# The first block's queries and keys loaded by head pairs in 2 KB rows, and turned by 64-column matmuls

## Chip, cores and metric

One core of a Trainium2 chip. The metric is device time in microseconds (us). The profiled span is about 1.8 us shorter than the device time of the same run, so differences may be read from either. In the lines of the profile PE is TensorE (PEld its weight loads), DVE is VectorE, ACT ScalarE, POOL GpSimd and SP SyncE; a load "lands" when its last count is posted.

For a program on one core, a run more than 1.5% above the fastest of the same kernel is called slow, and a difference of less than 2% is called "same".

## The reference

Attention over the last 128 positions and the first 4 ("sinks"), then a two-layer network on its result.

```python
# q, k, v: (4, 8, 768, 64) float32; w_in: (512, 2048); w_out: (2048, 512)
scores = q @ k.transpose(0, 1, 3, 2) / sqrt(64)
rel    = pos[:, None] - pos[None, :]
keep   = (pos[None, :] < 4) | ((rel >= 0) & (rel < 128))
a      = softmax(where(keep, scores, -1e9))
x      = (a @ v).transpose(0, 2, 1, 3).reshape(3072, 512)
h      = x @ w_in
out    = (h / (1 + exp(-1.702 * h))) @ w_out
```

## The kernel before

The 3072 tokens are worked on in 12 blocks of 256. For each block q and k are loaded, cast to fp16 and turned, so that the head dimension lies on the partitions; then come scores, exponentials, the product with v, and the two layers. A list scheduler inside the kernel puts all operations into one order per engine, using estimated durations. It also fills early gaps of TensorE with "warming" matmuls on zeros, which keep its clock up: between 14 and 16 us the granted clock is 0.50 in the changed kernel, and 1.00 in run 4, which adds more of them.

Block 0's q goes through SP's ring (its list of transfers) and its k through ACT's, each in two loads of 256 KB:

```python
def load(k):
    ...
    for e, src in enumerate((q, k_ap)):
        eng, dma = ("ACT", nc.scalar) if k == 0 and e else ("POOL", nc.gpsimd) if k == 2 else ("SP", nc.sync)
        if k < KT:                            # KT = 4: blocks 0 to 3
            for h in range(2):                # even heads, odd heads
                dma.dma_start(                # (called through the scheduler)
                    dst[:, e].rearrange("p h i d -> p (h i d)")[:, 512 * h : 512 * h + 512],
                    src[b, h::2, t0 : t0 + TB].rearrange("p (g i) d -> g p (i d)", i=8),
                )
    ... # v of the block, then the next block, behind these in SP's ring
```

Eight tokens of one head are contiguous in memory: 8 x 64 x 4 bytes = a row of 2 KB. In the source pattern `g` is the group of eight tokens (32 of them) and `p` the head of the half (4). Destination partition 4g + p takes one row. Each half, once cast, holds the even or odd heads alone, and turning works on an even and an odd head side by side, so it waits for both halves:

```python
def turn_on_pe(k, e, i, T, C, war):
    def tp():
        for a in range(4):                    # 128 columns: two heads of 64
            nc.tensor.transpose(f16(o_tp)[:, bass.ts(a, P)], C[:, a].rearrange("s h d -> s (h d)"), perm)
    o_tp = op("PE", ..., tp, [o_cqk[k, e, 0], o_cqk[k, e, 1], o_perm], ...)   # both halves
    ... # copies from PSUM to blkT, on DVE or ACT
```

`perm`, the identity with its columns in another order, undoes the order of the partitions. It is the moving operand; the data are what PE loads as weights (`LDWEIGHTS <-qk` in the trace).

The softmax here doesn't subtract the row's maximum and nothing guards it: scores larger than these inputs give would overflow.

## Time and profile before

Three runs gave 221.77 us (median; 221.62 to 227.12). The start, by when things happened in the profiled run (us from its start; landings from the semaphore records):

| event | us |
|---|---|
| block 0 lands: k half 1, q half 1, k half 2, q half 2 | 4.66, 5.33, 6.37, 7.04 |
| last cast of block 0 starts | 7.06 |
| first exponential starts | 9.44 |
| v of block 0, v of block 1 land | 11.73, 14.06 |
| first weight transfer lands | 16.41 |
| first matmul with w_out starts | 28.81 |
| end of the span | 220.0 |

The lines of the profile are in the prediction below.

### The profile page before, as it was taken

To read this page: it belongs to the slowest core of one execution; us is meant where nothing else is said; L and a number is where in the kernel's file an instruction comes from. 1 tells how busy PE (TensorE), PEld (TensorE's weight loads), DVE (VectorE), ACT (ScalarE), POOL (GpSimd) and SP (SyncE) were. 2 spreads that over 40 slices of the span, in tenths; PEclk is the share of its full clock that TensorE was granted. 3 is DMA by queue.
4 is the path that set the end of the run, shared out by engine and by line. 5 is a ranking of instruction groups with operands and counts; after the bars stand their busy time and mean duration, and the time that the engine had idled before them with its cause. 6 is when DMAs were issued, how large, how long until landed. Compare 5 with 4: busy or idle time off the path is not lost.

```text
span 220.0 us, 5209 instructions
## 1 busy us (share of the span) xinstructions
PE 213.7 (97%) x2066; PEld 143.8 (65%) x2066; DVE 125.9 (57%) x274; ACT 125.7 (57%) x243; POOL 87.0 (40%) x150
## 2 busy tenths in 40 slices
PE   7889999999999999999999999999999999999993
PEld 3448777577757766666666667657667666666642
DVE  2678855397826855656556664666465655634310
ACT  2597645777557576475485476466466486444320
POOL 2596431689971956704905727508500000000000
PEclk9999999999999999999999999999999999999998
DMA  5999999999979589289498589398541312231223
GB/s 162 355 236 204 207 302 202 324 302 289 210 141 240 143 182 295 51 166 297 103 205 240 73 204 250 84 213 232 106 91 47 71 27 48 52 68 26 51 48 95
DMA packets 65911, 36.54 MB, mean 166 GB/s; under 512 B 27968, under 2 KB 61120, under 8 KB 65888
## 3 DMA queue, kind: packets, MB, share of 16 engines
q1 hardware_dynamic: 60848, 30.19, 56.0%
q0 software_dynamic: 4592, 5.37, 12.9%
q10 hardware_dynamic: 448, 0.66, 1.1%
q8 instruction: 16, 0.26, 0.5%
q14 instruction: 7, 0.06, 0.1%
HBM read 27.56 MB, written 6.29 MB: 154 GB/s over the span
## 4 chain that ended last, share of the span: by engine, by line
PE 91%; DMA 4%; ACT 2%; SPq 1%; issue 0%; DVE 0%
PE bank L736 39%; PE bank L765 37%; PE bank L669 6%; PE bank L604 5%; DMA qk<-in_q_dram 3%; PE bank L532 1%; DMA out_dram<-osb 1%; ACT at L629 1%; ACT v L286 1%; PE bank L596 1%; PE bank L584 1%; PE bank L708 1%; SPq L407 0%; PE bank L846 0%; ACT blkT L286 0%
## 5 line engine op out<-in xcount | busy, mean ns | idle before, releaser
L765 PE MATMUL bank<-w_out,gT 128*128 128x512 f16 (+2 forms) x400 | 99.8, 371 | 0.0
L736 PE MATMUL bank<-xT,w_in 128*128 128x256 f16 x768 | 99.8, 273 | 0.0
L750 DVE SCALAR_TENSOR_TENSOR gT<-th,bank 128x512 f16<-128x512 f16 x96 | 65.5, 683 | 48.8 <-ACT th L748 47.8
L748 ACT ACTIVATE th<-bank 128x512 f16<-128x512 f32 x96 | 57.7, 603 | 62.0 <-PE bank L736 61.3
L736 PEld LDWEIGHTS <-w_in 128*128 128x128 f16 x768 | 72.9, 98 | 23.8 <-issue 1.7
L286 POOL CAST qk<-qk 64x512 f16<-64x512 f32 (+1 forms) x74 | 44.9, 609 | 45.1 <-DMA qk<-in_q_dram 41.9
L629 ACT ACTIVATE at<-bank 128x512 f16<-128x512 f32 (+1 forms) x96 | 48.7, 569 | 10.9 <-PE bank L604 10.9
L765 PEld LDWEIGHTS <-gT 128*128 128x128 f16 x400 | 36.1, 98 | 23.3 <-issue 1.4
L636 DVE TENSOR_TENSOR at<-at,bank 128x1024 f16<-128x1024 f16 (+1 forms) x40 | 25.7, 643 | 22.8 <-ACT at L629 22.8
L286 POOL CAST v<-v 64x512 f16<-64x512 f32 (+1 forms) x43 | 26.1, 606 | 8.9 <-DMA v<-in_v_dram 6.8
L669 PE MATMUL bank<-v,at 128*128 128x65 f16 x352 | 21.2, 193 | 0.1
L784 ACT ACTIVATE osb<-bank 128x512 f32<-128x512 f32 (+1 forms) x24 | 14.4, 600 | 11.0 <-PE bank L765 11.0
L669 PEld LDWEIGHTS <-at 128*128 128x128 f16 x352 | 17.5, 97 | 4.2 <-DVE at L636 0.3
L689 DVE TENSOR_TENSOR xb<-bank,rcp 128x256 f16<-128x256 f32 x36 | 15.2, 422 | 0.7
L669 PE MATMUL bank<-vs,ats 128*128 128x65 f16 x128 | 14.7, 193 | 0.0
L604 PEld LDWEIGHTS <-blkT 64*128 64x128 f16 x256 | 8.0, 94 | 9.3 <-issue 7.8
L604 PE MATMUL bank<-blkT 64*128 64x256 f16 x192 | 13.4, 244 | 0.0
L669 PEld LDWEIGHTS <-ats 128*128 128x128 f16 x128 | 12.0, 97 | 2.0
L687 DVE RECIPROCAL rcp<-bank 128x4 f32<-128x4 f32 x48 | 8.4, 177 | 3.6 <-PE bank L669 3.2
L286 ACT COPY blkT<-bank 128x256 f16<-128x256 f16 (+1 forms) x12 | 5.1, 463 | 4.4 <-PE bank L532 4.3
L604 PE MATMUL bank<-blkT,blkT 64*128 64x128 f16 x64 | 7.2, 222 | 0.0
L846 PE MATMUL bank<-zero 128*128 128x512 f16 x19 | 5.8, 463 | 1.2 <-DVE zero L304 1.2
(43 smaller groups left out, 68.4 us busy)
## 6 DMA issues: line engine op xcount, KB each, us to landing
v<-in_v_dram SPq DMA_DIRECT2D x12, 512.0 KB, 6.7
out_dram<-osb SPq DMA_DIRECT2D x46, 128.0 KB, 2.4
qk<-in_q_dram SPq DMA_DIRECT2D x8, 512.0 KB, 5.3
qk<-in_k_dram SPq DMA_DIRECT2D x8, 512.0 KB, 6.7
w_in<-in_moe_w_in_dram POOLq DMA_DIRECT2D x4, 512.0 KB, 9.5
w_out<-in_moe_w_out_dram POOLq DMA_DIRECT2D x4, 512.0 KB, 12.8
qk<-in_q_dram SPq DMA_DIRECT2D x6, 256.0 KB, 5.3
qk<-in_k_dram SPq DMA_DIRECT2D x4, 256.0 KB, 5.5
```

Of the source, the lines that this page charges most:

```text
L286: {"POOL": nc.gpsimd.tensor_copy, "DVE": nc.vector.tensor_copy, "ACT": nc.scalar.copy}[e](out=out, in_=in_)
L604: nc.tensor.matmul(f32(o_s, 2 * n + i)[:, c : c + w], src[d, j], Q[d].rearrange("d j s -> d (j s)")[:, q0 : q0 + w], start=k >= KM, stop=T ...
L629: nc.scalar.activation(out=A[:, i, 0:W], in_=f32(o_s, 2 * n + i)[:, 0:W], func=AF.Exp, scale=scale)
L636: nc.vector.tensor_tensor(out=A[:, :, 0:W], in0=A[:, :, 0:W], in1=mask(c0, c0 + W).unsqueeze(1).to_broadcast((P, 2, W)), op=ALU.mult,)
L669: nc.tensor.matmul(avp()[:, j, i], a_, v_, start=(n == 0), stop=(n == len(mms) - 1))
L687: o_r = op("DVE", 93, 190, lambda: nc.vector.reciprocal(out=rc, in_=avp()[:, :, :, D]), [o_a], prio=base - 1.2 * h8, kind="rcp")
L689: o_n = op("DVE", 340, 430, lambda: nc.vector.tensor_tensor(out=X, in0=avp()[:, :, :, 0:D], in1=rc.to_broadcast((P, 2, 2, D)), op=ALU.mult ...
L736: nc.tensor.matmul(f32(holder[0])[:, bass.ts(e, TB)], w_in16[:, c, bass.ts(Fi, P)], X[:, c] if k < KX else X2[:, :, c], start=(c == 0), st ...
L748: o_t = op("ACT", 477, 600, lambda first=first: nc.scalar.activation(out=th[first.places[0]], in_=f32(first), func=AF.Tanh, scale=0.851), ...
L750: o_g[k, s] = op("DVE", 590, 700, lambda first=first, s=s: nc.vector.scalar_tensor_tensor(out=g[:, 2 * s : 2 * s + 2].rearrange("p a t -> ...
L765: nc.tensor.matmul(f32(holder[0])[:, 0:w], g[:, Fi, bass.ts(j, P)], w_out16[:, Fi, c0:c1], start=(Fi == 0), stop=(Fi == NF - 1),)
L784: nc.scalar.mul(O[:, c0:c1], f32(holder[0])[:, 0:w], 0.5)
```

## The change

The intent: let the first head pairs start without waiting for the whole block. Each half now holds four adjacent heads (two pairs) instead of the even or odd ones, so a half can be cast in one contiguous piece and turned by itself. Since the two heads of a pair no longer lie side by side after the cast, each is turned by its own 64-column matmul. The core of the diff (block 0 only, `KN = 1`; planner settings and the unused `CD` option are cut):

```diff
+    perm8 = pool.tile([P, P], FP16, name="perm8")          # the old perm, for blocks 1 to 3
...
-        out=perm.rearrange("r (h g) -> r h g", h=NP), in_=ident.rearrange("r (g h) -> r h g", h=NP)),
+        out=perm.rearrange("r (h p g) -> r h p g", h=2, p=2), in_=ident.rearrange("r (p h g) -> r h p g", p=2, h=2)),
...
-            if k < KT:
+            if k < KN:
+                for y in range(2):
...
+                        return dma.dma_start(to, src[b, 4 * y : 4 * y + 4, t0 : t0 + TB].rearrange("h (g i) d -> h g (i d)", i=8))
...
+            elif k < KT:
...
+    def turn_halves(k, e, y, T, C, war):
+        def tp():
+            for i in range(8):
+                for h in range(2):
+                    d = slice(64 * h, 64 * h + 64)
+                    nc.tensor.matmul(
+                        f32(o_tp)[d, bass.ts(i, 64)], C[:, bass.ts(i, 64)], perm[:, d], start=True, stop=True,
+                    )
+        o_tp = op("PE", TPN, TPN + 170, tp, [o_cqk[k, e, y], o_perm], prio=base, acq=("t", 1), kind="tp")   # one half
...
+        for t in range(2):
+            ... # two copies of 128 x 256 from PSUM to blkT, on DVE or ACT
```

The source pattern was `g p (i d)`, 32 x 4 x 512, and is now `h g (i d)`, 4 x 32 x 512.

More of the change, by code (lines that the diff above doesn't have):

```diff
@@ L229 @@
     KT, KX, AHEAD = globals().get('OPT',{}).get('KT',4), 3, globals().get('OPT',{}).get('AHEAD',0)
+    KN = globals().get('OPT',{}).get('KN',1)
     RB, KM = 4, globals().get('OPT',{}).get('KM',2)
@@ L302 @@
     OPT = globals().get("OPT", {})
+    CD, TPN = OPT.get("CD", ()), OPT.get("TPN", 550)
     VS_AT = NEVER + 14.505
@@ L330 @@
     o_perm = op("POOL", 330, 450, lambda: nc.gpsimd.tensor_copy(
-        out=perm.rearrange("r (h g) -> r h g", h=NP), in_=ident.rearrange("r (g h) -> r h g", h=NP)),
+        out=perm.rearrange("r (h p g) -> r h p g", h=2, p=2), in_=ident.rearrange("r (p h g) -> r h p g", p=2, h=2)),
         [o_ident], prio=NEVER, kind="const")
+    o_perm8 = op("POOL", 330, 450, lambda: nc.gpsimd.tensor_copy(
+        out=perm8.rearrange("r (h g) -> r h g", h=NP), in_=ident.rearrange("r (g h) -> r h g", h=NP)),
+        [o_ident], prio=NEVER+3, kind="const")
     def no_sinks():
@@ L352 @@
     OPT = globals().get("OPT", {})
+    CD, TPN = OPT.get("CD", ()), OPT.get("TPN", 550)
     CAST_QK = ["DVE ACT", "POOL DVE"] + ["POOL"] * (NK - 2)
@@ L388, in eights, with halves @@
         return c16.rearrange("s i e h d -> s (i e h d)").rearrange("s (e i a h d) -> s e i a h d", e=2, i=2, a=4, h=2)
+    def halves(c16):
+        return c16.rearrange("s i e h d -> s (i e h d)").rearrange("s (e y n) -> s e y n", e=2, y=2)
     o_cqk, o_cv, o_vs = {}, {}, {}
@@ L401, in load, with f @@
         for e, src in enumerate((q, k_ap)):
-            eng, dma = ("ACT", nc.scalar) if k == 0 and e else ("POOL", nc.gpsimd) if k == 2 else ("SP", nc.sync)
+            eng, dma = ("ACT", nc.scalar) if k == 0 and e else ("POOL", nc.gpsimd) if k == 2 or k in CD else ("SP", nc.sync)
             lq[e] = []
-            if k < KT:
+            if k < KN:
+                for y in range(2):
+                    def f(e=e, y=y, src=src, dma=dma):
+                        to = halves(qk16[k % RQ])[:, e, y] if k in CD else dst[:, e].rearrange("s h i d -> s (h i d)")[:, 512 * y : 512 * y + 512]
+                        return dma.dma_start(to, src[b, 4 * y : 4 * y + 4, t0 : t0 + TB].rearrange("h (g i) d -> h g (i d)", i=8))
+                    lq[e].append(op(eng, 780 if k in CD else 450, (850 if k == 3 and k not in CD else 700, 8), f, war + (reuse("qk16", k % RQ) if k in CD else []),
+                                    prio=prio + y / 2 + (1 - e) / 8, kind="load"))
+            elif k < KT:
                 for h in range(2):
@@ L432, in load @@
         c16 = qk16[k % RQ]
-        war = reuse("qk16", k % RQ)
+        war = [] if k in CD else reuse("qk16", k % RQ)
         if k >= KT:
@@ L443, in load, with f @@
                         o_cqk[k, 2 * e + j, i] = o
+        elif k in CD:
+            for y in range(2):
+                for e in range(2):
+                    o_cqk[k, e, y] = lq[e][y]
+        elif k < KN:
+            C = halves(c16)
+            for y in range(2):
+                for e in range(2):
+                    def f(eng, e=e, y=y):
+                        copy(eng, C[:, e, y], dst[:, e].rearrange("s h i d -> s (h i d)")[:, 512 * y : 512 * y + 512])
+                    o_cqk[k, e, y] = plan.any(cast(512, CAST_QK[k] if k != 1 else "DVE ACT" if y else OPT.get("Q1", "POOL")), f, [lq[e][y]] + war,
+                                              prio=nominal(k - 1, -7 + 2 * y) if k else NEVER + y, kind="cqk")
         else:
@@ L452, in load @@
                                               prio=nominal(k - 1, -7 + 2 * h) if k else NEVER + h, kind="cqk")
-        for o in {id(x): x for (kk, _, _), x in o_cqk.items() if kk == k}.values():
+        for o in {id(x): x for (kk, _, _), x in o_cqk.items() if kk == k and k not in CD}.values():
             uses("s32", sl, o)
@@ L503, in turn @@
         o_t = []
-        if k < KT:
+        if k < KN:
+            for y in range(2):
+                two = [x for e in (1, 0) for x in turn_halves(k, e, y, T, halves(c16)[:, e, y], war)]
+                o_t.append(two)
+                for p in (2 * y, 2 * y + 1):
+                    o_qkT[k, p] = two
+        elif k < KT:
             for i in range(2):
@@ L509, in turn @@
             o_t.append(turn_by_dma(k, T, slots(c16), war))
-        for p in range(NP):
+        for p in range(NP) if k >= KN else ():
             o_qkT[k, p] = [o[p] for o in o_t]
@@ L525, in turn, with f @@
                 o_ks[b, p] = o
+    def turn_halves(k, e, y, T, C, war):
+        base = attend(k, 0) - 5 * L / 8 + 2 * y + e
+        def tp():
[6 more added lines that the diff above has]
+        o_tp = op("PE", TPN, TPN + 170, tp, [o_cqk[k, e, y], o_perm], prio=base, acq=("t", 1), kind="tp")
+        uses("qk16", k % RQ, o_tp)
+        out = []
+        for t in range(2):
+            def f(eng, t=t):
+                copy(eng, T[:, e, 2 * y : 2 * y + 2].rearrange("d p j (t g a) -> d t (p j) g a", t=2, a=4)[:, t],
+                     f32(o_tp).rearrange("d (a t n g) -> d t n g a", a=4, t=2, n=4)[:, t])
+            out.append(plan.any({"DVE": (330, 440), "ACT": (275, 390)}, f, [o_tp] + war,
+                                prio=base - (OPT.get("CP", L) if k == 1 else 0), kind="cp"))
+        out[1].rel = [(o_tp, 0)]
+        out[1].deps.append(out[0])
+        return out
     def turn_on_pe(k, e, i, T, C, war):
@@ L531, in tp @@
             for a in range(4):
-                nc.tensor.transpose(f16(o_tp)[:, bass.ts(a, P)], C[:, a].rearrange("s h d -> s (h d)"), perm)
-        o_tp = op("PE", 4 * pe_ns(P), 3 * pe_ns(P) + P / 2.4 + 166, tp, [o_cqk[k, e, 0], o_cqk[k, e, 1], o_perm],
+                nc.tensor.transpose(f16(o_tp)[:, bass.ts(a, P)], C[:, a].rearrange("s h d -> s (h d)"), perm8)
+        o_tp = op("PE", 4 * pe_ns(P), 3 * pe_ns(P) + P / 2.4 + 166, tp, [o_cqk[k, e, 0], o_cqk[k, e, 1], o_perm8],
                   prio=base + 2 * i + e, acq=("t", 1), kind="tp")
```

## The prediction

Its load term stands on the estimate from the counts in the trace of before. There the sink loads of v, whose outermost dimension is 8, post 8 counts, and block 0's loads, with 32, post 16; so loads whose source begins with 4 were taken to go over 4 DMA engines, the same four for all of block 0's; "each" and "the four" below are these engines. That a source alone can do this was not shown before the change ran. The half speed in the clock term is an estimate too: the sign of it in the trace of before is the warming matmuls, first 0.43 us apart and later 0.22. What the 64-column matmuls would cost PE (rival C) had no measurement behind it.

> **What bounds the kernel now.** I read the page's top and its chain that ended last first: they say whether a change at the start can reach the end.
>
> ```profile
> span 220.0 us, 5209 instructions
> PE 213.7 (97%) x2066; PEld 143.8 (65%) x2066; DVE 125.9 (57%) x274; ACT 125.7 (57%) x243; POOL 87.0 (40%) x150
> ...
> PE   7889999999999999999999999999999999999993
> ```
>
> PE is busy in nearly every slice, and 91% of the chain is PE. So the span is the time until dense PE work begins plus a fixed amount of PE work. The change touches only the first block, so the chain in order of time, cut to 0 to 40 us, comes next (start, length, what):
>
> ```profile
> 1.49 5.55 DMA qk<-in_q_dram
> 7.04 0.02 issue
> 7.06 0.44 DVE qk L286
> ...
> 11.08 0.86 ACT at L629 x2
> ...
> 15.95 0.50 ACT at L629
> ...
> 19.04 0.87 PE bank L736 x8
> ```
>
> The second half of q of block 0 lands at 7.04. Then cast, turning, scores, and from 9.44 to 17.4 a nearly full ACT; from 16.5 the chain is PE alone, with the first MLP matmuls (L736) at 18.9. From 16.5 on PE has nothing to give back: a delay or a gain of this start reaches the end almost whole. The timeline from 0 shows which waits pace the start:
>
> ```profile
> 4.68 0.43 DVE L286 CAST qk<-qk 128x512 f16<-128x512 f32 x1 [2.87 <-DMA qk<-in_k_dram]
> ...
> 5.74 0.29 POOL L330 COPY perm<-const 128x128 f16<-128x128 f16 x1 [3.26 <-DMA const<-const]
> ...
> 7.06 0.43 DVE L286 CAST qk<-qk 128x512 f16<-128x512 f32 x1 [0.24 <-DMA qk<-in_q_dram]
> ...
> 11.75 1.07 DVE L286 CAST v<-v 64x256 f16<-64x256 f32 x3 [0.51 <-DMA v<-in_v_dram]
> ```
>
> Casts start as loads land, and v's too. Last, the DMA side in one-microsecond windows; the last two columns are the DMA share and GB/s:
>
> ```profile
> 4.00:5.00 1.00, 1.00 (x6) 0.49 (x5) 0.32 (x1) 0.00 (x0) 0.00 (x0) 1.00 1.05 410
> 5.00:6.00 1.00, 1.00 (x6) 0.29 (x3) 0.53 (x2) 0.00 (x0) 0.26 (x1) 1.00 1.06 408
> 6.00:7.00 1.00, 0.26 (x4) 0.13 (x3) 0.43 (x1) 0.00 (x0) 0.03 (x1) 1.00 1.05 365
> ```
>
> All 16 DMA engines are full from 4 us. The packet records have 84 ns for a row of 2 KB, also at 3 to 4 us, when the share was only 0.67: a limit of one engine, not of the memory. The landings agree: the loads of block 1 (256 KB, 128 rows, 8 rows an engine) land at 7.77, 8.44, 9.12 and 9.87, 0.67 apart, and 8 x 84 ns is 0.67.
>
> [...] the sink loads of v have 8 as outer dimension, and their semaphores show one jump at issue (6.84) and 8 single counts (11.15 to 11.87), where each 128-row load shows 16. For the same reason the view of DMA issues has no landing time for them:
>
> ```profile
> v<-in_v_dram SPq DMA_DIRECT2D x1, 512.0 KB, 6.7
> ...
> vs<-in_v_dram SPq DMA_DIRECT2D x4, 8.0 KB
> ```
>
> [...] The trace has no 64-column weights; 128x128 weights with 65-column matmuls go at 30 ns a pair (12 in 0.36 us). [...]
>
> **The change, part by part.** *Loads.* Both versions move 2 KB rows, 128 a load, four loads. The source of before is "g p (i d)": 32 x 4 x 512; after it is "h g (i d)": **4 x 32 x 512**. [...] Each gets 32 rows a load instead of 8: 24 x 84 ns = 2.0 us more, and four loads make 8.1 us. Twelve engines get nothing from these loads, but every later transfer (block 1's q and k, v, the mask constants, weights) is cut over all 16 and waits for its share on the four. Before, the first rows start at 2.2 and about 1.5 us go in starting up; after: 2.2 + 1.5 + 128 x 0.084 = 14.5, plus 0.5 for the last count: the last half lands near **14.5 to 15** instead of 7.04. SP's and ACT's rings alternate, so the first half lands near 9, not 5.3. Block 1's k follows by 2.0 (as 7.04 to 9.12 now), v by 4.7 (7.04 to 11.73), hence v near 19.5. The first weight transfer is issued after block 1's k (9.42 against its landing at 9.12) and lands 7.0 later, now 16.41; it goes to about 24, the later ones with it. Shift of the whole start: 7.4 to 8.1 us.
>
> *Casts.* Four of 0.43 us, contiguous now; the last still trails its load. No gain.
>
> *Turning.* 16 matmuls of 128 columns (16 x 56 ns = 0.9 us) become 64 of 64 columns[...]. Half lies ahead of the second load, hidden. [...] only half of the copies follow (two of 0.42 on DVE, 0.84, against 1.27)[...].
>
> *Order.* I compared the instruction order of the two built programs. PE still runs all four turning units before the first scores, so the first head pairs do not start early: the intended gain is mostly ordered away. After some 30 us of work the order is the same on every engine. ACT gets one cast of block 1 ahead of its first exponential (it waits for block 1's k), one more copy of block 1 and two more copies of x, and one less of block 0: 0.49 + 0.37 + 0.6 - 0.32 = 1.1 us on an engine that was full from 9.4 to 17.4. Perhaps half shows: +0.5. *Clock.* Warming matmuls fall from 19 to 13 and end by about 5.5. Then PE waits to 9, works for 1 to 2 us and waits to 15[...], so turning and first scores may run at half speed: their 1.0 to 1.5 us cost 0.5 to 1 more.
>
> **Sum.** 7.7 (loads) + 0.5 (ACT) + 0.7 (clock) = 8.9, of which nearly all arrives at the end, as PE has no slack after the start: 221.8 + 8.9 is about **230.5 us**, 4% slower.
>
> **The rivals.** *A: 16 engines after all*, if the split goes by the 128 destination rows. For it: no transfer in this trace has an outer source dimension unlike its destination's[...]. Then the first units wait for perm (6.03) and fit before the second half's cast (7.49), the last turn ends near 8.1, the copies near 8.8; scores come up to 0.6 earlier, but ACT's cast waits for k at 9.12 and ends at 9.6, after the 9.44 of its first exponential now, and has 1.1 us more to do. Result 221 to 223, same. *B: 4 engines, but mostly hidden*, because v and weights have twelve free engines and the start has slack. Against it: a transfer is done only when all its engines are, and the chain has no idle time between the load and dense PE; the first weights land at 16.41 against use at 18.9, 2.5 us of slack, which helps only if attention catches up. ACT's full stretch says it doesn't. If it did: +5, 227. *C: the turning binds*: [...] It adds a little to the main reading, since half is hidden. *D: the delay compounds*, with PE cold until the MLP is dense, or weights falling behind: +11 to 13, 233 to 235.
>
> **Range and chances.** I hold the four-engine reading at 0.87; within it 227 to 234 is nearly everything (B at the low end, D at the high). A takes most of the rest and lies within 2% (217.3 to 226.2). Faster by 2% would need 4.4 us off a start whose load cannot come sooner: 0.01. Slower 0.86, same 0.13. Range 227 to 234.
>
> **What would show it.** In the changed profile: the loads of q and k of block 0 take about 8 us (first) and 12 to 13 us (second) from issue to landing instead of 3.9 and 5.5; DMA share in the windows from 4 to 9 us drops to well under 1 and GB/s towards 100 once the other engines have drained; the last cast of block 0 starts near 15; the v cast near 19.5; first MLP matmuls near 27; from there the rest as long as before (some 201 us). If 2 KB loads still land 0.67 apart and the cast is at 7.06, A is right and I am wrong. If the start is late by 8 but the end by less than 5, B. [...] a doubled spacing after 15 us, the clock term.

## The result, and the profile after

The changed kernel takes **232.78 us** (median of 4 runs, 232.32 to 233.98), beside 222.12 for the kernel before (4 runs, one of them slow at 227.12 and left out of the ratio). The ratio is 1.050, 95% interval 1.044 to 1.055: slower. Ratios here are the mean time of one kernel's fast runs over that of the other's of the same rounds, so not quite the ratio of the medians quoted.

The page's top for the changed kernel; the two rows are TensorE's busy share and its granted clock, in tenths, in 40 slices:

```profile
span 230.9 us, 5291 instructions
...
PE   7039899999999999999999999999999999999994
...
PEclk9755999999999999999999999999999999999999
```

TensorE is idle nearly throughout the second slice (5.8 to 11.5 us), and its clock is at half in the third and fourth. From there on the rows look as before. The page's DMA issues, first before, then after (the last figure is the median time from issue to landing):

```profile
qk<-in_q_dram SPq DMA_DIRECT2D x6, 256.0 KB, 5.3
```

```profile
qk<-in_q_dram SPq DMA_DIRECT2D x6, 256.0 KB, 14.8
```

The row must be read with care. Its median is of those transfers whose landing the view can tell, and block 0's are not among them: before, they are one of block 1's and one of block 3's; after, one of block 1's alone (issued at 2.96, landed at 17.73). So it shows how long a load behind block 0's now takes. Block 0's own two q loads took 4.6 and 5.6 us before (issued at 0.74 and 1.49) and 12.0 and 14.9 after (0.74 and 1.54), by the landings of the tables. What the DMA view of 0 to 30 us says of block 0's k is that after the change it has no landing with 16 counts any more (first before, then after):

```profile
qk<-in_k_dram ACTq DMA_DIRECT2D x2, 256.0 KB, 3.9
```

```profile
qk<-in_k_dram ACTq DMA_DIRECT2D x2, 256.0 KB
```

The timeline of DVE shows the four casts of block 0, with what ended the idle time before each:

```profile
8.76 0.43 DVE L288 CAST qk<-qk 128x512 f16<-128x512 f32 x1 [6.95 <-DMA qk<-in_k_dram]
12.78 0.43 DVE L288 CAST qk<-qk 128x512 f16<-128x512 f32 x1 [3.60 <-DMA qk<-in_q_dram]
14.74 0.43 DVE L288 CAST qk<-qk 128x512 f16<-128x512 f32 x1 [1.53 <-DMA qk<-in_k_dram]
16.42 0.43 DVE L288 CAST qk<-qk 128x512 f16<-128x512 f32 x1 [1.25 <-DMA qk<-in_q_dram]
```

They still trail their loads, and the last starts at 16.42 instead of 7.06. The windows say why (columns: window and its length, busy time and count of PE, PEld, DVE, ACT and POOL, then granted clock, DMA share, GB/s):

```profile
9.00:10.00 1.00, 0.00 (x0) 0.00 (x0) 0.18 (x1) 0.00 (x0) 0.34 (x1) 0.50 0.31 109
...
14.00:15.00 1.00, 0.33 (x14) 0.19 (x8) 0.26 (x1) 0.59 (x2) 0.00 (x0) 0.50 0.26 98
15.00:16.00 1.00, 0.64 (x16) 0.51 (x16) 0.17 (x1) 0.10 (x1) 0.00 (x0) 0.50 0.26 98
20.00:22.00 2.00, 2.00 (x15) 1.07 (x14) 1.40 (x5) 1.21 (x4) 1.84 (x6) 0.50 0.99 265
22.00:24.00 2.00, 2.00 (x27) 1.11 (x27) 1.12 (x4) 1.90 (x5) 1.85 (x4) 0.92 1.24 206
```

In 14 to 16 us the DMA share is 0.26, about 4 of 16, and the rate 98 GB/s is 4 times 2048 bytes in 84 ns (24.4 GB/s). The clock column reads 0.50 until 22 us. The semaphore records agree: each of block 0's four loads now shows one jump at issue and then 4 single counts, where before each showed 16. The rows of ACT's queue (q10) in the DMA view of 0 to 30 us show the same by the number of packets, 288 before and 264 after for the same bytes:

```profile
q10 hardware_dynamic: 288, 0.52, 6.4%
```

```profile
q10 hardware_dynamic: 264, 0.52, 5.9%
```

Both have 256 data rows; what is left is 2 x 4 = 8 counts instead of 2 x 16 = 32. Last, the chain that ended last, from its start (start, length, what):

```profile
1.54 14.86 DMA qk<-in_q_dram
16.42 0.44 DVE qk L288
16.90 0.64 PE bank L569 x10
...
21.99 0.49 ACT at L688
...
29.11 0.54 PE bank L795 x4
...
39.87 0.86 PE bank L824 x4
```

It is the chain of before with a longer first piece. L795 is the first layer and L824 the second; the piece that answers to the last line is, in the chain of before:

```profile
28.98 0.86 PE bank L765 x4
```

39.87 - 28.98 = 10.89, and the two spans differ by 10.9. So the whole loss is there before the second layer starts, and nothing is lost or won back later.

| event (us) | after | shift |
|---|---|---|
| block 0 lands: k half 1, q half 1, k half 2, q half 2 | 8.73, 12.76, 14.71, 16.40 | 4.1, 7.4, 8.3, 9.4 |
| last cast of block 0 starts | 16.42 | 9.36 |
| first exponential starts | 18.96 | 9.5 |
| v of block 0, v of block 1 land | 20.84, 23.20 | 9.1, 9.1 |
| first weight transfer lands | 26.13 | 9.7 |
| first matmul with w_out starts | 39.70 | 10.89 |
| end of the span | 230.9 | 10.9 |

### The profile page after: what moved, and what is told of

It reads as the page before. It is cut to its first block, busy times and chain, and to the rows that moved or that the text cites. A ratio compares the mean times of both kernels' runs of the same rounds, so it can differ in the third digit from the quotient of the medians.

```text
span 230.9 us, 5291 instructions
## 1 busy us (share of the span) xinstructions
PE 216.4 (94%) x2108; PEld 144.8 (63%) x2108; DVE 124.8 (54%) x271; ACT 127.0 (55%) x246; POOL 88.0 (38%) x151
## 4 chain that ended last, share of the span: by engine, by line
PE 88%; DMA 7%; DVE 1%; ACT 1%; SPq 1%; issue 0%
PE bank L795 37%; PE bank L824 35%; DMA qk<-in_q_dram 6%; PE bank L728 6%; PE bank L663 5%; PE bank L655 2%; PE bank L591 1%; DMA out_dram<-osb 1%; PE bank L643 1%; PE bank L767 1%; ACT v L288 1%; DVE xn L748 0%; SPq L418 0%; PE bank L569 0%; ACT osb L843 0%
## 5 line engine op out<-in xcount | busy, mean ns | idle before, releaser
L795 PE MATMUL bank<-xT,w_in 128*128 128x256 f16 x768 | 100.1, 273 | 0.0
L824 PE MATMUL bank<-w_out,gT 128*128 128x512 f16 (+2 forms) x400 | 99.8, 371 | 0.0
L795 PEld LDWEIGHTS <-w_in 128*128 128x128 f16 x768 | 72.8, 98 | 24.0 <-issue 1.9
L824 PEld LDWEIGHTS <-gT 128*128 128x128 f16 x400 | 36.1, 98 | 23.3 <-issue 1.4
L663 PE MATMUL bank<-blkT 64*128 64x256 f16 x192 | 13.9, 250 | 0.0
L569 PE MATMUL bank<-perm,qk 128*64 128x64 f16 x64 | 2.3, 243 | 9.0 <-DVE qk L288 9.0
L288 DVE CAST qk<-qk 128x512 f16<-128x512 f32 x5 | 2.3, 452 | 14.1 <-DMA qk<-in_k_dram 9.3
L569 PEld LDWEIGHTS <-qk 128*64 128x64 f16 x64 | 1.9, 154 | 9.8 <-DVE qk L288 9.8
```

The source lines that it names most:

```text
L288: {"POOL": nc.gpsimd.tensor_copy, "DVE": nc.vector.tensor_copy, "ACT": nc.scalar.copy}[e](out=out, in_=in_)
L663: nc.tensor.matmul(f32(o_s, 2 * n + i)[:, c : c + w], src[d, j], Q[d].rearrange("d j s -> d (j s)")[:, q0 : q0 + w], start=k >= KM, stop=T ...
L795: nc.tensor.matmul(f32(holder[0])[:, bass.ts(e, TB)], w_in16[:, c, bass.ts(Fi, P)], X[:, c] if k < KX else X2[:, :, c], start=(c == 0), st ...
L824: nc.tensor.matmul(f32(holder[0])[:, 0:w], g[:, Fi, bass.ts(j, P)], w_out16[:, Fi, c0:c1], start=(Fi == 0), stop=(Fi == NF - 1),)
```

## The experiments

The theory: the four loads of block 0 are carried by 4 DMA engines instead of 16, because the outermost dimension of their source went from 32 to 4; they land 9 us later, and that passes on to the end. The rivals: the turning by 64-column matmuls or the new order costs the time; or the clock does. Nine kernels were run, one of them a second time; all gave the right result. "Before" medians beside them were 221.88 (runs 1 to 4), 221.84 (5 to 7, and the repeat of 3) and 221.68 (8, 9).

**1. The change with the old outermost dimension.** Everything is kept (head pairs, contiguous casts, 64-column matmuls), only partition 4g + h takes what partition 32h + g took:

```diff
-  src[b, 4 * y : 4 * y + 4, t0 : t0 + TB].rearrange("h (g i) d -> h g (i d)", i=8)
+  src[b, 4 * y : 4 * y + 4, t0 : t0 + TB].rearrange("h (g i) d -> g h (i d)", i=8)
-  perm ... in_=ident.rearrange("r (p h g) -> r h p g", p=2, h=2)
+  perm ... in_=ident.rearrange("r (g p h) -> r h p g", p=2, h=2)
```

> The changed kernel with only the access pattern of the four loads of block 0 turned to 32 x 4 x 512 (group outermost) and the permutation matrix to match; instruction order the same on every engine. Theory (the outer dimension of 4 puts each load on 4 DMA engines, and that is the whole loss but for what follows from it): each of the four loads posts 16 counts and takes 0.67 us of the queues, the last lands at 7.0 to 7.4, the first MLP matmul starts near 19 to 19.5, and the run is 221.5 to 223.5 us, ratio to before 0.998 to 1.007. Rival 1 (the 64-column turning and the new order cost several us by themselves): the loads are quick but the run stays at 225 us or more. Rival 2 (the rows are slow for where they lie in memory, not for the number of engines): can't be told from the theory by this run alone.

Measured: 222.18 us (221.95 to 222.25, 6 runs), ratio 1.000 (0.998 to 1.003), same. The loads count to 16 again. Two lines of its timeline:

```profile
6.67 0.43 DVE L288 CAST qk<-qk 128x512 f16<-128x512 f32 x1 [0.27 <-DMA qk<-in_q_dram]
...
6.85 1.20 PE L569 MATMUL bank<-perm,qk 128*64 128x64 f16 x64
```

The last cast is even a little earlier than in the trace of before (6.67, against 7.06); so it is in run 9 (6.63), which has the old loads, so this is no gain of the change. All 64 turning matmuls take 1.20 us. Everything that the change does besides the loads costs nothing that this run can resolve. It also gains nothing: PE was busy with warming matmuls until 6.85, so the early first half lay unused. The first scores came at 8.41, but ACT cast block 1's k first (8.70), so the first exponential started at 9.23, 0.82 after them; in the kernel before it is 0.37 (9.07 to 9.44).

**2. The kernel before with an outermost dimension of 4 in block 0.** The reverse: the old halves, casts and transposes, with only the loads' order changed.

```diff
-  src[b, h::2, t0 : t0 + TB].rearrange("p (g i) d -> g p (i d)", i=8)
+  src[b, h::2, t0 : t0 + TB].rearrange("p (g i) d -> p g (i d)" if k == 0 else "p (g i) d -> g p (i d)", i=8)
-  transpose(..., perm)
+  transpose(..., ident if k == 0 else perm)
```

> The kernel before with only the four loads of block 0 turned to 4 x 32 x 512 (and the identity in place of the permutation for that block). 128-column turning, even and odd heads, order as before. Theory: the load term alone; 4 counts a load, last landing near 16.4 as in the changed kernel, first MLP matmul near 28.5 to 29, run 231 to 233 us (ratio 1.04 to 1.05). Rival 1 (turning and order carry much of the loss): 226 to 229 us.

Measured: 233.17 us (232.32 to 234.21, 4 runs), ratio 1.050 (1.046 to 1.054): the whole loss, without any other part of the change. Its chain begins as the changed kernel's does:

```profile
1.53 15.72 DMA qk<-in_q_dram
```

The profile fell on the slowest of the four runs (234.21): the last load landed at 17.26 where 16.4 was expected, and the first matmul with w_in came at 31.3 instead of 28.5 to 29.

Runs 1 and 2 together settle the main point: the order of the loads' source is necessary and sufficient for the loss. They don't tell apart the rival that run 1's text names, rows that are slow for where they lie in memory; the packet records do. A row takes 84 ns (median) in the kernel before, and 84 to 88 in the new order when nothing else moves (run 5): it is their number per engine that grew.

**3. Only the second halves on 4 engines** (first halves as in run 1, second halves as in the change, each with its own permutation). This asks whether the loss follows the landing of the last load, or the work of the four engines.

```diff
+  .rearrange("h (g i) d -> h g (i d)" if y else "h (g i) d -> g h (i d)", i=8)
+  matmul(..., (perm if y else perm0)[:, d], ...)
```

> The changed kernel with the 4-row outer dimension kept only on the second halves (q and k of head pairs 2, 3); the first halves go 32 x 4 x 512. One more copy of a permutation matrix on POOL (0.3 us, beside the load). Theory: half the extra rows on the four engines, 2 x 24 x 84 ns = 4.0 us, so the last half lands at 11 to 12 and the run is 226 to 228.5 us, about midway between e1_outer32 and the changed kernel. Rival (the loss is not in proportion to the rows per engine, for example a fixed stall of the queues as soon as one load is uneven): near 232 or near 222.

Measured: 237.73 and 238.27 (slow), 229.19 and 229.86 (fast); ratio of the fast ones 1.034 (1.029 to 1.038). The expectation of 226 to 228.5 was missed. The profile fell on a slow run, in which q's second half on SP's ring landed at 11.08, as the sum says, but k's second half on ACT's ring only at 14.35. Two pieces of its chain:

```profile
1.47 12.89 DMA qk<-in_k_dram
...
16.77 12.41 DMA v<-in_v_dram
```

Between 11 and 14 us, by the packet records, k's rows took turns with the next transfers of SP's ring, block 1's q (landed at 12.85 and 14.16). So the last landing (14.35) comes later than the rows of block 0 alone would make it. If it was the same in the fast runs, which have no trace, it explains them: 14.35 - 7.04 = 7.3, and their spans (227.2 and 227.8) are 7.2 and 7.8 longer than 220.0. The second line is what this slow run waited for: v of block 1, issued at 16.77 behind the first weights (15.13), lands at 29.2. That this sets slow runs apart from fast ones is not shown. A repeat for one look took 238.13 and was again of this kind:

> The same kernel as e3_second_only, whose profile fell on one of its two slow runs (237.7 us), for a look at a fast one (229.2 and 229.9). Theory (the end moves with the last landing, which was 14.35 there): last landing near 14.3, first MLP matmul near 26, run 229 to 230. If it falls slow again (237 to 239), block 1's v lands near 29 as in that profile, behind weights.

No trace of a fast run was had, so why the same program falls to one side or the other stays open.

**4. The change, kept warm.** Warming matmuls are added ahead of the turning units (31, 3 and 4), so that the clock never falls.

```diff
+  for _ in range({(0, 0): 31, (1, 1): 3, (0, 1): 4}.get((e, y), 0)):
+      warm(None)
```

> The changed kernel with 38 more warming matmuls of zeros in PE's waits for the loads (31 before the first turning unit, 3 and 4 before the third and fourth). Theory (the halved clock from 9 to 22 us costs a part of the 1.3 us by which the loss exceeds the late landing): granted clock 1.0 to 22 us, landings as in the changed kernel (16.4), turning, masks and first scores at full speed, 0.7 to 1.5 us quicker: 231.3 to 232.1 us. Rival (the start is paced by ACT and by v and weights, so PE's clock does not matter there): within 0.3 us of the changed kernel.

Measured: 232.05 us (232.03 to 232.13, 4 runs), ratio 1.045 (1.041 to 1.049). Its windows, to be laid beside those of the changed kernel:

```profile
14.00:16.00 2.00, 1.43 (x38) 0.73 (x31) 0.43 (x1) 0.65 (x2) 0.00 (x0) 1.00 0.26 97
20.00:22.00 2.00, 1.71 (x19) 0.89 (x19) 1.81 (x6) 1.98 (x6) 1.90 (x5) 1.00 0.88 220
```

The clock is at 1.00, the DMA share at 0.26 as before. In this profiled run the last landing was 0.4 later, which hides some of the gain; the cast's start shows it:

```profile
16.81 0.43 DVE L288 CAST qk<-qk 128x512 f16<-128x512 f32 x1 [1.26 <-DMA qk<-in_q_dram]
```

From there to the first matmul with w_out (38.99) it is 22.18 us; in the changed kernel 39.70 - 16.42 = 23.28. So the half clock costs 1.10 us between these two traces (the medians of the two kernels are 0.73 apart). In the kernel before the same stretch is 28.81 - 7.06 = 21.75, and in run 1 it is 28.87 - 6.67 = 22.20. The 0.43 between 21.75 and 22.18 is left for turning and order, and the chains say that it is PE's order: PE is the chain from 16.49 on before and from 25.75 on in run 4. That is 9.43 and 8.94 us after the last cast, so the part of ACT and DVE ahead of it became shorter; but from there to the first matmul with w_out it is 12.32 and 13.24, so more of PE's work is left for then. Run 1 has the same 8.96 and 13.24.

**5. The change with the next loads held back.** Block 1's first load (and with it all of SP's ring) waits until block 0 has landed. The sum had 14.5 to 15 for the last landing and the trace 16.40; if the other traffic slows the four engines, that gap must close.

```diff
+  gates.append((o_first[0], o_b0[-1]))     # block 1's first load waits for k half 2 ...
+  gates.append((o_first[0], o_b0[1]))      # ... and q half 2 of block 0
```

> The changed kernel, its four 4-engine loads as they are, with block 1's first load held on SP until both second halves of block 0 have landed; what SP issues after it waits too. It tests why the last half landed at 16.4 and not at the 14.5 to 15 of the sum. Theory (rows on the four engines go slower, 100 to 135 ns instead of 84, while the other twelve move block 1 and v): with nothing else on the queues the rows take 84 to 88 ns throughout and the last half lands at 14.8 to 15.3. Rival (the four engines are slow of themselves, for where they write or for their full rings): it lands at 16 to 16.6 as before. The end is no measure here: block 1 and v come later by 1 to 2 us, so 233 to 235 us under both.

Measured: four runs of 237.44, 234.60 (fast), 238.96 and 240.74 (slow), ratio 1.064 (1.058 to 1.070). The end was expected at 233 to 235 and missed: v of block 1 lands after 28 us. But the disputed point is clear, from its chain and its windows:

```profile
1.54 13.21 DMA qk<-in_q_dram
```

```profile
8.00:10.00 2.00, 0.00 (x0) 0.00 (x0) 0.09 (x1) 0.00 (x0) 0.23 (x1) 0.99 0.26 98
10.00:12.00 2.00, 0.55 (x20) 0.55 (x22) 0.43 (x1) 0.00 (x0) 0.00 (x0) 0.50 0.26 98
```

The last half lands at 14.75, and a row takes 84 to 88 ns from 3 us on. In the changed kernel the rows of ACT's queue took 100 to 135 ns on average at 5 to 9 and 11 to 13 us, while the other twelve engines moved block 1 and v, and 84 to 88 when alone. So the 16.40 is the sum's 14.75 plus 1.65 of slowing by other traffic. Where that happens (memory, or a path the engines share) no run here tells. The amount of traffic alone is not it: in the kernel before rows took 84 ns (median) at 4 to 6 us with all 16 engines full, at 408 to 410 GB/s, while here it was 203 to 317 at 5 to 9 us.

**6. What the change was meant for.** Run 1 with 9 warming matmuls instead of 13 ahead of the turning, the first half's copies on ACT and the second's on DVE, and block 1's k cast by DVE alone, so that ACT is free for the first exponential.

```diff
-  while t + 300 < s:                                    # warming matmuls
+  while t + (1500 if s < 6000 else 300) < s:
-  plan.any({"DVE": (330, 440), "ACT": (275, 390)}, f, [o_tp] + war,
+  plan.any({"DVE": (420, 500)} if y else {"ACT": (330, 430)}, f, [o_tp] + war,
-  cast(512, CAST_QK[k] if k != 1 else "DVE ACT" if e else ...)
+  cast(512, CAST_QK[k] if k != 1 else "DVE" if e else ...)
```

> e1_outer32 (loads on 16 engines) with what kept the first half from being used taken away: 9 warming matmuls instead of 13, so that PE is free when the first casts end; copies of the first half on ACT and of the second on DVE; block 1's k casts on DVE alone, so that ACT's first exponential does not stand behind a load. Theory (the halves are worth something once the order lets them through): first turning at 5.7 to 6.0 instead of 6.85, first exponential at 8.0 to 8.4 instead of 9.2, run 221.0 to 221.7, 0.2 to 0.5 per cent quicker than before. Rival (v, which lands near 11.3, and PE's fixed work from 16 us on pace the start whatever the first scores do): within 0.3 us of e1_outer32, 221.9 to 222.5, or slower if fewer warming matmuls leave PE cold.

Measured: 223.37 us (222.09 to 225.84, 6 runs, two of them slow), ratio 1.004 (1.000 to 1.008). The first exponential starts at 8.24, 1.2 us earlier than before, and nothing comes of it: the 221.0 to 221.7 us that were expected are missed. In the profiled run (224.4) the chain passes not through ACT but through a load, v of block 1, which landed at 15.69:

```profile
8.90 6.79 DMA v<-in_v_dram
```

The weights, issued at 8.88, ran beside it. PE, which had waited too, then ran at half clock: the windows of 16 to 18 and 18 to 20 us read 0.68 and 0.50. The run's mean clock is 0.990, that of the two runs of 222.1 us 1.000.

**7. Block 1's k cast by DVE alone**, on top of run 1 (the last of the three edits of run 6, by itself).

> e1_outer32 with one part of that alone: block 1's k casts on DVE only, which also puts one more exponential ahead of the v casts on ACT. Theory: first exponential at 8.7 to 8.9 instead of 9.2, run 221.6 to 222.1. Rival: same as e1_outer32, 222.0 to 222.4.

Measured: 223.79 us (222.12 to 226.05, 6 runs, two slow), ratio 1.007 (1.003 to 1.010). The first exponential starts at 8.31, and again the end is not earlier (221.6 to 222.1 was expected). But 8.31 is not this edit's doing alone: of the same 13 warming matmuls the later ones ran 0.22 us apart here and 0.43 in run 1's trace, so they ended at 5.59 instead of 6.92, and the turning began at 5.67 instead of 6.85.

**8. Run 6 with the weights later**: the first weight transfer waits for the last of block 1's q and k loads instead of the one before it.

```diff
-  g = o_first[OPT.get("WG", -2)]
+  g = o_first[OPT.get("WG", -1)]
```

> e6_intent with the first weight transfer waiting for block 1's last load instead of its last but one (0.7 us later). In e6_intent's profile the first exponential did come 1.2 us sooner (8.24), but block 1's v landed at 15.7, behind weights that had started sooner, and DVE, ACT and PE waited 1.3 to 1.5 us for it. Theory (the gain of the halves is lost to that race and comes out once v goes first): v of block 1 lands by 14.2, no slow tail of runs, 221.0 to 221.7 us. Rival (PE's work from 16 us on and v of block 0 pace it anyway): 221.8 to 222.4, only the spread goes.

Measured: 221.74 us (221.56 to 221.92, 5 runs), ratio 1.000 (0.999 to 1.001). The spread of runs 6 and 7 is gone and the gain is nil; the time lies between what the theory (221.0 to 221.7) and the rival (221.8 to 222.4) had. Its chain shows what took the place of the wait that was removed:

```profile
8.92 5.89 DMA v<-in_v_dram
14.84 0.42 DVE v L288
15.29 0.30 DVE xT L288
...
29.07 0.86 PE bank L824 x4
```

and ACT's timeline the early exponential:

```profile
8.24 1.64 ACT L688 ACTIVATE at<-bank 128x384 f16<-128x384 f32 x4 [0.96 <-PE bank L663]
```

ACT begins 1.2 us earlier than before, but v of block 1 lands at 14.81 (by 14.2 was expected), and PE is the chain from 15.6 on. The first matmul with w_out comes at 28.91, against 28.81 before. Even here PE ran the second half's turning ahead of the first scores: the exponential is early because the scores as a whole are (7.87 instead of 9.07; it follows them by 0.37 in both kernels), not because the first pairs go first. The last cast was 0.48 earlier in this trace, and the three warming matmuls that stand between turning and scores in the kernel before (8.00 to 8.81) are gone.

**9. The kernel before with the weights later** (the same edit by itself), to see whether run 8 owes anything to it.

> The control: the kernel before with that later first weight transfer alone. Theory (before, the weights have no effect on the start but in its slow runs): 221.5 to 222.1, and no run above 223. Rival (the weights are needed that early): slower by up to 0.7 us.

Measured: 222.68 us (222.14 to 224.88, 6 runs), ratio 1.006 (1.003 to 1.009): within 2%, but not the equality that was expected, and two runs lie above 223. Its profile fell on the longest run, 224.88, where one 64 x 256 cast of v on DVE took 2.29 us (the two others of its form 0.29 and 0.38), so it says little of the others. What held the cast is open: an operation of POOL on vs ran beside it from 13.71 to 14.78 and the cast ended at 14.94, but no run tests a link. No kernel beats the one before; runs 1 and 8 equal it.

## Why the prediction was right

It said 230.5 us (227 to 234; its terms add up to 221.8 + 8.9 = 230.7) and slower; measured 232.78. The sizes of the sum's terms can be checked one by one against the span's 10.9. The loads and the clock were both taken too small, so their errors add up and put the time near the top of the range. That the third term fits is luck: the point on order below says why.

| term of the sum | predicted | measured | from |
|---|---|---|---|
| loads | 7.7 | 9.36 | start of the last cast, 7.06 to 16.42 |
| clock | 0.7 | 1.10 | 23.28 - 22.18 (run 4) |
| ACT and order | 0.5 | 0.43, but by PE's order | 22.18 - 21.75 (run 4) |
| sum | 8.9 | 10.89 | |

- **Four engines.** Right: 4 counts a load, 98 GB/s, a share of 0.26, and runs 1 and 2. One sign came only in part: the DMA share of the windows from 4 to 9 us was to drop to well under 1, and was 0.67, 1.00, 1.03, 0.80 and 0.67, as the twelve other engines were still moving block 1; it is 0.26 when they have drained. Rival A, that the 128 destination rows would decide, is refuted. What it foresaw for 16 engines, 221 to 223, is what run 1 measured.
- **When the last half lands.** This is the mis-sized term: "the last half lands near 14.5 to 15" was 16.40. The sum took 84 ns for every row; run 5 shows that this holds when the four engines work alone (14.75), and that other transfers cost the rest. The trace of before gave no hint of it: its rows took 84 ns with all 16 engines full.
- **The first half near 9.** Right for k (8.73), wrong for q (12.76). In the kernel before the halves of the two rings land in turn (k 4.66, q 5.33, k 6.37, q 7.04); here the two rings did not alternate evenly. SP's first row moved at 4.33, ACT's at 2.19, and by 8.75 ACT's queue had moved 153 packets, all of k's first half (128 rows) and the start of its second, so q's first half had had fewer turns.
- **What is behind the loads.** v landed at 20.84 (19.5 predicted), the first weights at 26.13 (24), the first matmuls with w_in at 29.0 (27): each later by 1.3 to 2.1 us, about what the last landing was (1.4 to 1.9). Block 1's loads, themselves of 16 counts, show the wait for the four engines: its k has 12 counts by 8.38, the other 4 come from 17.78 on, and it lands at 18.41 instead of 9.12.
- **The order.** Right: PE ran all four turning units before the first scores, and ACT's cast of block 1's k (18.43) came ahead of its first exponential (18.96). The cost put on it was right in size and wrong in reason: the prediction had half of ACT's 1.1 us of added work show; in run 4 the part of ACT and DVE is 0.49 shorter than before, and 0.92 more of PE's work comes after it.
- **Turning.** Rival C, that it binds, is refuted: run 1 has all the turning and no loss (222.18 us, ratio 1.000). There, at full clock, the 64 matmuls take 1.20 us, of which one by itself is 0.20, so the 32 pairs of column halves go by about every 32 ns, 1.0 us in all, about as much as 16 of 56 ns before. At half clock, in the changed kernel, pairs are 53 ns apart, and the two halves of a pair start 0 to 7 ns apart.
- **Mostly hidden (rival B).** Refuted: the landing's 9.36 arrived whole at the first matmul with w_out, and from there both kernels need the same 191.2 us (220.0 - 28.81 and 230.9 - 39.70).
- **Compounding (rival D).** In part: the cold clock is its share, 1.10 instead of 0.7. It came sooner than predicted, not between the two turnings: the clock fell at 8.69, ahead of the first turning and 2.5 us after the last warming matmul had ended (6.17, not "about 5.5"), and rose at 22.34. A second load falling far behind is not seen in the changed kernel, but it is in runs 3 and 5, where v of block 1 lands after 28 us.

Why the intended gain is absent even with 16 engines is answered only in part. Run 8 shows that an exponential 1.2 us earlier meets the load of v of block 1. The version that was meant, in which PE works on the scores of the first pairs before the second half is turned, was not reached: the scheduler put the turning first in every kernel whose order was looked at.

## What to carry to other kernels

When a load's pattern is rewritten, look at the outermost dimension of both sides before looking at row length: 2 KB rows to 128 partitions went from 16 DMA engines to 4 because the source alone began with a dimension of 4 (16 counts a load against 4, runs 1 and 2). The four engines that carried the urgent load made what stood behind it in the ring late too (v of both blocks by 9.1 us), so read the landings of the next transfers as well as its own. And if an early wait is removed, ask which load ends last after it: here it was v of the next block, and 1.2 us of earlier exponentials were worth nothing.
